# Idle TensorE products in pairs, the first keys fetched before the first queries, and a new table of order

## The chip, the cores and the metric

The kernel runs on one core of a Trainium2 chip. The metric is the device time of one execution in microseconds (us). Three executions of the kernel before took 779.79, 780.46 and 781.97 us, so the median is 780.46 us. A profiled execution has its own time, given below.

## The reference

Hashed attention over 2 batches, 8 heads, 768 positions and a head width of 64, followed by two feed-forward layers on the 1536 resulting tokens, all in 32-bit floats:

```
q_bits, k_bits = (q @ proj > 0), (k @ proj > 0)        # 6 bits each -> a bucket number
scores = where(q_bucket == k_bucket, q @ k.T / sqrt(64), -1e9)
attn   = softmax(scores);  x = attn @ v                # tokens x 512
h = x @ w_in;  g = h if h >= 1, 0 if h <= -1, else (h + 1)**2 / 4
y = g @ w_out                                          # 512 -> 2048 -> 512
out = ((y @ w_a) * (y @ w_b)) @ w_out2                 # 512 -> 1536 -> 512
```

## The kernel before, in words

Every 32-bit operand of a large product is split into a high and a low part, and three products stand for one (high by high, high by low, low by high). The split is two instructions: a rounding copy (line L372 on VectorE and GpSimd, L370 on ScalarE) and a subtraction (L375 on VectorE or GpSimd).

Attention of batch 0 runs first, in tiles of 128 queries by 768 keys. For each head: load the keys (`kn`, L395) and queries (`qnh`, L384); copy the keys beside themselves (`kn<-kn`, L372); split the queries (`qsh`); transpose keys (`tk`, L488) and queries (`tq`, L528) on TensorE and evict them (`kh`, `kl`, `qt`); form the hash signs (`kp`, L561; `bit`, L566) and the bucket rows (`kid`, L579, L613, L614; then `q2`, printed as `q`, L622, and the upper half of `kl`, L588). A tile of scores is four products (`s`, L673), a row minimum on VectorE (`mn`, L677) and an exponential on ScalarE (`sm`, L679). It is then split into `phi` and `plo`, turned by DMA (L707) and multiplied by the values in groups of 36 products (`pv`, L746). There are 96 tiles and 48 groups of values.

As soon as blocks of 384 tokens of batch 0 are complete (`xn`), they are transposed (`xt`, L1012), split into `xsh` and `xsl`, and the first feed-forward layer starts (`hp`, L1044; `acc`, L1256). Its products fill TensorE between the attention tiles of batch 1. The second layer follows (`mx`, `mz`, `acc`, L1177, and the output product L1282). Weights arrive as raw words (`stage`, L937) and are put together on ScalarE and VectorE (`wab`, `F`, L940 to L946).

Nothing schedules this at run time. Every step is recorded as an operation with the engines that may take it. The string `ORDER` gives, for each operation in turn, the engine (p, a, v, g or s) and the distance in the list to the next operation. It therefore fixes the order on each engine's queue, and which engine takes a step that several can take. Each engine runs its queue in order. SyncE (SP) issues the DMAs, also in order. Buffers are handed out from pools in that same order: `kn` has one buffer, so the next head's keys can be requested only when both `tk` steps of this head are done.

At the start TensorE gets products that compute nothing (`idle<-warm`): eight at L1340, and eight more from `keep_busy` (L473), which `tq` calls around the first head's query transposition. In the kernel before, the latter are two operations, one of six products and one of two. The first score tile of the program is recorded as waiting for these operations (`after=idle_mm`).

Of the kernel before, what the change touches and what calls it, by code (L numbers as in the profile page):

```python
# [39 lines left out]
a46 v19 v17 s-49 a38 a24 p-23 a-11 p16 v p v2 g15 a-16 s-23 p9 a10 v-3 g-15 p39 a g-23 g13 v11 p a v p-17 v a-12  # L40
p36 a58 g2 a-59 v136 s-184 s201 a68 p-227 a-18 a48 v-7 g8 s-72 v184 v-165 v23 v112 p-106 s-9 g a9 s-24 p3 v s-3
p50 v v a-51 a18 g-1 g9 v-75 p95 a v-44 a13 g13 a198 p-194 a v14 s174 a-187 g3 p-15 v p244 p-237 v v237 v v-277
a32 g17 p-12 p32 a s-11 a p-14 v4 g14 s-30 a196 v-183 p55 a v p-43 v a119 a-133 p51 a-36 s8 p a a24 g v133 v-131
v v81 v a-116 g11 p-4 p5 a p a a s-48 p33 v7 s-10 p47 a p-26 s18 v-28 v13 v-2 a-12 p38 v-29 g8 a52 s-79 g80 a100
s-40 p-99 v a7 p13 p2 v-1 v3 v-1 a-42 s2 p3 v a16 s-19 g18 a-1 a17 p-6 g-14 p41 a a59 v-86 a v-26 v53 p g-27 g20
s24 s-43 p16 v s-16 a26 v p-25 p26 v v54 a-66 g2 g12 p9 a v31 g g-63 p35 p108 a-119 s448 v-398 a-54 a19 p-6 v111
p-119 v11 v2 g17 s-33 a12 p6 v105 p-103 a2 a-1 v-2 p28 v a22 g p-41 g-1 a-14 v60 p-22 a g-18 s-35 s94 v-64 a p10
v p-6 v v p47 s-52 a12 g-1 g13 p-3 v a-12 g17 p2 s-28 v29 p a31 v g-5 v-26 a-9 v11 a g12 v-53 a119 a-60 p-9 v
p-17 a5 p26 a p10 v s50 a v p-33 v-26 v60 v-33 s-66 a21 s8 p11 v v26 p-20 a-22 a19 a33 v s-77 p25 g17 v7 s-27
a19 a11 p31 p-5 v6 p s-62 p30 a33 p34 v-41 a v-33 a v6 v p46 v s42 a-17 g-46 g-51 p37 a v g13 g46 s-78 a95 v v  # L50
s-31 a5 v-17 a-1 v-15 a29 v v s-68 a56 v18 p-55 a a-15 g a15 v p16 p33 a-32 a a35 g6 p-24 a s-4 v-31 v p37 p26
a-28 g v-19 p58 s32 a v-60 a a-31 g298 s-285 a47 g a-19 v49 v a-46 v12 s8 a p-31 v a v-37 v74 v-7 v p-48 a26 v
s-8 a36 g20 p-26 a p-51 p2 p43 p-1 s-5 a45 s-63 a40 g p-10 v a s59 v-28 s-99 p56 p p14 v p-23 v s56 a-69 v p49
a6 v20 a-70 g p71 v-27 a28 a41 g a-30 s-37 s-18 p21 s-2 a3 a-6 g25 a-113 v128 p-52 a a a28 v23 v17 p-37 p11 g27
v-37 a v-32 v28 a-27 g p35 a a4 p9 p-28 s50 v-19 s p5 p-38 s57 v-85 v35 v28 g8 p-41 p a14 a22 v-9 a s3 s40 p-38
a-38 v20 a19 p3 v a-20 v a30 g-8 s19 v-1 v-9 g-54 a43 v-19 g v30 p14 a p11 a a-11 p-11 v v11 a-13 p-8 p33 a v-90
a67 g4 v33 a-32 v p-19 p-1 p2 a23 g p27 a-1 s-17 a-7 p20 v p-7 a-4 g p25 v35 v-70 v a20 v4 s-37 p26 a19 v a2
s-21 a17 p-6 v a g9 v v16 a-38 v33 g s-9 s117 v-141 p28 v p-34 v6 p-7 a47 p-56 a a52 p-4 v a-13 a3 v34 a-23 v-10
p13 a p6 p19 a v-54 v15 p24 a s-39 s34 a47 v-71 v19 a25 v g27 p-52 p p s15 p-4 a-8 s23 p6 a v-15 p-9 v3 p32 v-34
# [207 lines left out]
def attn_moe_kernel(ctx: ExitStack, tc: tile.TileContext, q, k, v, proj,  # L267
                    w_in, w_out, w_a, w_b, w_out2, consts, codes, out):
    nc = tc.nc
# [20 lines left out]
    HJ = J // 2  # L290
# [41 lines left out]
    add = pr.add  # L332
# [19 lines left out]
    warm = const.tile([128, 1], BF16, name="warm")  # L352
# [112 lines left out]
    busy = {}  # L465
# [932 lines left out]
```

## Time and profile before

| | |
|---|---|
| median of three runs | 780.46 us |
| the profiled execution's own time | 783.63 us |
| its span, first to last instruction | 781.8 us |
| TensorE busy | 755.3 us, 97% |
| VectorE busy | 666.1 us, 85% |
| ScalarE busy | 488.6 us, 62% |
| GpSimd busy | 374.5 us, 48% |
| mean granted TensorE clock | 0.993 of full speed |

Busy is time in which an engine executes. Times of rows are counted from the start of the span. In a row of the timeline, the square bracket says how long the engine sat idle before the row and which instruction ended that. PE is TensorE, DVE VectorE, ACT ScalarE, POOL GpSimd, and SPq is SyncE issuing a DMA.

### The profile page before, as it was taken

To read this page: it belongs to the slowest core of one execution; us is meant where nothing else is said; L and a number is where in the kernel's file an instruction comes from. 1 tells how busy PE (TensorE), PEld (TensorE's weight loads), DVE (VectorE), ACT (ScalarE), POOL (GpSimd) and SP (SyncE) were. 2 spreads that over 40 slices of the span, in tenths; PEclk is the share of its full clock that TensorE was granted. 3 is DMA by queue.
4 is the path that set the end of the run, shared out by engine and by line. 5 is a ranking of instruction groups with operands and counts; after the bars stand their busy time and mean duration, and the time that the engine had idled before them with its cause. 6 is when DMAs were issued, how large, how long until landed. Compare 5 with 4: busy or idle time off the path is not lost.

```text
span 781.8 us, 14714 instructions
## 1 busy us (share of the span) xinstructions
PE 755.3 (97%) x5532; PEld 698.5 (89%) x5532; DVE 666.1 (85%) x1176; ACT 488.6 (62%) x897; POOL 374.5 (48%) x333
## 2 busy tenths in 40 slices
PE   7888799999999999999999999999999999999998
PEld 5677699999989999989999999999999889999986
DVE  5999999999988888889977776899889996988764
ACT  5897799899998886766435433464546663443223
POOL 1667566445584667662234235253143165543630
PEclk9999999999999999999999999999999999999999
DMA  7899999999989867773022321023531103122011
GB/s 240 179 208 219 200 247 239 221 233 223 206 170 179 160 133 110 124 112 95 29 76 59 108 82 54 27 82 111 152 114 55 40 1 95 55 89 73 1 41 40
DMA packets 202791, 95.50 MB, mean 122 GB/s; under 512 B 165216, under 2 KB 197216, under 8 KB 202720
## 3 DMA queue, kind: packets, MB, share of 16 engines
q1 hardware_dynamic: 202272, 94.39, 53.0%
q8 instruction: 43, 0.70, 0.4%
q14 instruction: 28, 0.23, 0.1%
q10 hardware_dynamic: 448, 0.17, 0.1%
HBM read 53.65 MB, written 3.15 MB: 73 GB/s over the span
## 4 chain that ended last, share of the span: by engine, by line
PE 81%; DVE 11%; ACT 4%; issue 3%; DMA 1%; POOL 0%; SPq 0%; DVEq 0%; ACTq 0%; POOLq 0%
PE hp L1044 16%; PE acc L1256 15%; PE acc L1282 12%; PE mx L1177 12%; PE s L673 7%; PE mz L1177 6%; PE pv L746 5%; PE acc L1177 3%; DVE mn L677 2%; PE kp L561 2%; ACT sm L679 1%; DMA kn<-in_k 1%; PE tq L528 1%; DVE plo L375 1%; PE tk L488 1%
## 5 line engine op out<-in xcount | busy, mean ns | idle before, releaser
L375 POOL TENSOR_TENSOR plo<-sm,phi 128x768 f16<-128x768 f32 x55 | 95.0, 1730 | 33.9 <-ACT phi L370 24.1
L677 DVE TENSOR_REDUCE mn<-s 128x1 f32<-128x768 f32 x96 | 91.2, 952 | 15.8 <-PE s L673 14.9
L679 ACT ACTIVATE sm<-s,mn 128x768 f32<-128x768 f32 x96 | 86.2, 899 | 24.6 <-DVE mn L677 20.1
L1230 ACT ACTIVATE t<-hp,half 128x384 f32<-128x384 f32 x64 | 36.9, 577 | 62.4 <-PE hp L1044 61.8
L673 PE MATMUL s<-kh,qt 128*128 128x384 f32 x192 | 72.5, 378 | 2.5 <-ACT sm L679 2.1
L375 POOL TENSOR_TENSOR wlo<-F,whi 128x512 fp32r<-128x512 f32 x39 | 54.0, 1385 | 41.9 <-ACT whi L370 22.5
L673 PE MATMUL s<-kl,q 128*128 128x384 f32 x192 | 66.8, 348 | 0.5 <-DVE q L622 0.5
L1282 PE MATMUL acc<-whi,gl 128*128 128x512 f32 x144 | 56.7, 394 | 0.0
L1282 PE MATMUL acc<-wlo,gh 128*128 128x512 f32 x144 | 56.6, 393 | 0.0
L1282 PE MATMUL acc<-whi,gh 128*128 128x512 f32 x144 | 56.0, 389 | 0.0
L375 POOL TENSOR_TENSOR gl<-t,gh 128x384 fp32r<-128x384 f32 x23 | 27.8, 1207 | 55.8 <-DVE gh L372 46.4
L1044 PE MATMUL hp<-xsh,whi 128*128 128x384 f32 x152 | 51.8, 341 | 1.5 <-DVE xsl L375 1.2
L1256 PE MATMUL acc<-gh,whi 128*128 128x384 f32 x144 | 51.8, 360 | 0.0
L746 PE MATMUL pv<-vc,pth 128*128 128x65 f16 (+1 forms) x1152 | 51.2, 194 | 0.1
L1044 PE MATMUL hp<-xsh,wlo 128*128 128x384 f32 x152 | 50.9, 335 | 0.0
L1044 PE MATMUL hp<-xsl,whi 128*128 128x384 f32 x152 | 50.9, 335 | 0.0
L746 PEld LDWEIGHTS <-pth 128*128 128x128 f16 x1152 | 41.9, 98 | 7.4 <-issue 6.5
L1256 PE MATMUL acc<-gl,whi 128*128 128x384 f32 x144 | 48.4, 336 | 0.0
L1256 PE MATMUL acc<-gh,wlo 128*128 128x384 f32 x144 | 48.4, 336 | 0.0
L1239 DVE SCALAR_TENSOR_TENSOR t<-t,hp 128x384 f32<-128x384 f32 x64 | 35.1, 548 | 15.2 <-ACT t L1235 12.2
L370 ACT ACTIVATE whi<-F 128x512 fp32r<-128x512 f32 x71 | 44.2, 624 | 3.6 <-issue 1.7
L370 ACT ACTIVATE phi<-sm 128x768 f16<-128x768 f32 x53 | 44.1, 841 | 1.5 <-DMA pth<-phi 0.9
(257 smaller groups left out, 2547.1 us busy)
## 6 DMA issues: line engine op xcount, KB each, us to landing
stage<-in_moe_w_out SPq DMA_DIRECT2D x31, 512.0 KB, 4.2
stage<-in_moe_w_a SPq DMA_DIRECT2D x17, 512.0 KB, 3.6
stage<-in_moe_w_b SPq DMA_DIRECT2D x17, 512.0 KB, 3.6
stage<-in_moe_w_in SPq DMA_DIRECT2D x16, 512.0 KB, 4.4
kn<-in_k SPq DMA_DIRECT2D x16, 192.0 KB, 3.7
out<-ob SPq DMA_DIRECT2D x12, 256.0 KB, 2.1
vn<-in_v SPq DMA_DIRECT2D x4, 384.0 KB, 5.1
vscan<-in_v SPq DMA_DIRECT2D x4, 384.0 KB, 4.5
```

What stands on the lines that cost most here:

```text
L370: nc.scalar.activation(dst, src, ACTF.Copy)
L375: (nc.vector if e == "dve" else nc.gpsimd).tensor_tensor(dst, a, b, ALU.subtract)
L673: nc.tensor.matmul(s()[:, i, 0:HC], x()[:, qs], t[i]()[:, 0:HC], start=(n == 0), stop=(n == 1))
L677: add({"dve": c_dve(S)}, lambda e: nc.vector.tensor_reduce(mn(), s()[:, :, 0:HC], AX.XY, ALU.min), r=[s], w=[mn])
L679: o = add({"act": c_act(S, True) + 0.093}, lambda e: nc.scalar.activation(sm().rearrange("p (c n) -> p c n", c=2), s()[:, :, 0:HC], ACTF.E ...
L746: nc.tensor.matmul(o[:, t, 0:D + 1 - i], w()[:, t, c, :], vcs[t]()[:, c, (1 - i) * D:(2 - i) * D + 1 - i], start=(n == 0), stop=(n == 3 * ...
L1044: nc.tensor.matmul(o()[:, 0:TB], a()[:, kk, :], m(), start=(n == 0), stop=(n == 3 * KD - 1))
L1177: nc.tensor.matmul(view()[:, 0:TB], a()[:, sl], m(), start=(start and n == 0), stop=(n == 5), skip_group_check=not start)
L1230: add({"act": 0.465}, lambda e: nc.scalar.activation(t(), o()[:, 0:TB], ACTF.Relu, bias=half, scale=0.5), r=[o], w=[t])
L1239: add({"dve": c_dve(TB)}, lambda e: nc.vector.scalar_tensor_tensor(t(), t(), 1.0, o()[:, 0:TB], ALU.min, ALU.max), r=[o], w=[t])
L1256: nc.tensor.matmul(ac()[:, 0:TB], a()[:, d, :], x(), start=(f == 0 and n == 0), stop=(f == F1 - 1 and n == 2))
L1282: nc.tensor.matmul(ac(), a()[:, ts], x().rearrange("p k n -> p (k n)"), start=(f == 0 and n == 0), stop=(f == F2 - 1 and n == 2))
```

## The change

`keep_busy` now records one operation for every two idle products, so that each pair has its own place in the table. The counts fall from six and two products to three pairs and one pair, which is the same eight products. Everything else is the new table.

```diff
-    NB1, NB2 = 6, 2
+    NB1, NB2 = 3, 1
...
         def mm(e):
-            for i in range(n):
-                nc.tensor.matmul(busy["t"][:, i % 2], warm.to_broadcast([128, 128]), warm.to_broadcast([128, 512]),
+            for i in range(2):
+                nc.tensor.matmul(busy["t"][:, i], warm.to_broadcast([128, 128]), warm.to_broadcast([128, 512]),
                                  start=True, stop=True)
-        idle_mm.append(add({"pe": 0.22 * n}, mm, w=[zz], after=[after]))
+        for i in range(n):
+            idle_mm.append(add({"pe": 0.44}, mm, w=[zz], after=[after]))
...
-s3 v3 v p10 s-16 v a17 v-14 p6 p-3 a v a2 p4 s11 v-14 v15 s3 a s-28 v40 s250 p-274 a p-3 p6 a2 p-4 v v2 g20 a250
+s s2 v3 v p12 a2 v-19 p9 s18 s4 v-28 p3 p8 a-4 v a-4 v p12 s-18 v42 p-29 g30 v-17 p-12 a5 p3 v8 v-6 a-1 p-3 v
```

The table is new from its first entry to its last (3512 entries before, 3514 now). TensorE executes the same products. In the whole program the copy `kn<-kn` goes from 10 times on GpSimd, 5 on ScalarE and 1 on VectorE to 5, 9 and 2; `phi` from 28, 53 and 15 to 22, 63 and 11; `plo` from 55 on GpSimd and 41 on VectorE to 58 and 38. The new source is one line longer in the table and one in `keep_busy`, so line numbers below grow by one or two.

On TensorE at the opening, from the key transposition of the first head (`tk`) to that of the second, the kernel before has the following (of each run of like rows, one stands):

```order
L488 MATMUL tk<-cst,kn 128x128 x6
L473 MATMUL idle<-warm 128x512
L561 MATMUL kp<-qt,zq_h 103x384
L561 MATMUL kp<-kl,zk 103x384
L473 MATMUL idle<-warm 128x512
L579 MATMUL kid<-bit,code 128x384
L614 MATMUL kid<-bit,code 64x384
L488 MATMUL tk<-cst,kn 128x128 x6
```

Here the first idle row stands six times and the second twice. Now the same place reads:

```order
L490 MATMUL tk<-cst,kn 128x128 x6
L474 MATMUL idle<-warm 128x512
L563 MATMUL kp<-qt,zq_h 103x384
L563 MATMUL kp<-kl,zk 103x384
L474 MATMUL idle<-warm 128x512
L581 MATMUL kid<-bit,code 128x384
L616 MATMUL kid<-bit,code 64x384
L474 MATMUL idle<-warm 128x512
L490 MATMUL tk<-cst,kn 128x128 x6
```

The idle rows stand two, four and two times. Four of the six products ahead of `kp` moved: two to the place behind it, and two behind the last `kid`, ahead of the second head's transposition.

On SyncE the program of before begins with:

```order
L384 DMA qnh<-in_q 128x192
L395 DMA kn<-in_k 128x6x64
L414 DMA vn<-in_v 128x2x384 x2
L384 DMA qnh<-in_q 128x192
L937 DMA stage<-in_moe_w_in 128x4x256
L395 DMA kn<-in_k 128x6x64
```

It now begins with:

```order
L396 DMA kn<-in_k 128x6x64
L385 DMA qnh<-in_q 128x192
L415 DMA vn<-in_v 128x2x384 x2
L385 DMA qnh<-in_q 128x192
L939 DMA stage<-in_moe_w_in 128x4x256
L396 DMA kn<-in_k 128x6x64
```

The first two have changed places; the next four stand as they did. On VectorE the first queries are still split before the keys are copied.

On VectorE, where the second piece of the first token block is split (`xsh`, `xsl`), the kernel before has:

```order
L372 CAST xsh_1219<-xt 128x384
L677 TENSOR_REDUCE mn<-s 128x1
L375 TENSOR_TENSOR plo<-sm,phi 128x768
L375 TENSOR_TENSOR xsl_1220<-xt,xsh_1219 128x384
L622 TENSOR_SCALAR q_1286<-kid,cst 128x384
L542 TENSOR_SCALAR qt<-tq 128x384
```

Now there is:

```order
L645 SCALAR_TENSOR_TENSOR vc<-vn,up_69,vc 128x6x64 x2
L373 CAST xsh_1227<-xt 128x384
L376 TENSOR_TENSOR xsl_1228<-xt,xsh_1227 128x384
L679 TENSOR_REDUCE mn<-s 128x1
L590 TENSOR_SCALAR kl<-kid 64x384
L544 TENSOR_SCALAR qt<-tq 128x384
```

The row minimum and the subtraction `plo` no longer stand between the two halves of the split; two subtractions for the values (`vc`) stand ahead of it.

## Rows read from the trace of the kernel before

**Rows 1.** Windows: start:end, length, each engine's busy us, clock, DMA share, GB/s.
```profile
0.00:20.00 20.00, 15.11 (x63) 10.05 (x63) 12.09 (x37) 11.84 (x23) 3.58 (x9) 0.91 0.74 235
20.00:97.00 77.00, 64.94 (x686) 52.26 (x686) 72.39 (x114) 63.81 (x108) 51.30 (x49) 0.96 1.04 203
97.00:125.00 28.00, 28.00 (x264) 26.38 (x265) 27.28 (x40) 26.13 (x49) 17.31 (x13) 1.00 1.10 245
125.00:600.00 475.00, 469.67 (x3624) 447.74 (x3621) 409.88 (x733) 309.69 (x568) 223.69 (x195) 1.00 0.56 126
600.00:782.00 182.00, 177.57 (x905) 162.07 (x903) 144.48 (x256) 77.14 (x153) 78.59 (x68) 1.00 0.14 47
```

**Rows 2.** Timeline of PE: start, length, row, idle before.
```profile
11.94 1.54 PE L488 MATMUL tk<-cst,kn 128*128 128x128 f32 x6 [1.49 <-POOL kn L372]
...
20.00 0.52 PE L488 MATMUL tk<-cst,kn 128*128 128x128 f32 x3 [1.20 <-POOL kn L372]
...
72.87 0.30 PE L528 MATMUL tq<-eye,qsh 128*128 128x128 f32 x1 [2.03 <-DVE xsl L375]
...
86.54 0.55 PE L1012 MATMUL xt<-cst,xn 128*128 128x128 f32 x3 [1.43 <-DVE q L622]
```

**Rows 3.** Windows, the stretch behind the first of these.
```profile
11.98:15.39 3.41, 3.41 (x14) 3.41 (x15) 2.18 (x5) 1.86 (x5) 0.00 (x0) 0.50 0.51 171
```

**Rows 4.** Line L677 with who waits for whom on DVE, 20 to 97 us: total, times, longest.
```profile
DVE mn L677 <- PE s L673: 1.6, 4, 1.0
```

**Rows 5.** The opening: chain of waits, PE timeline, SyncE timeline, landing times of `qnh`.
```profile
1.19 3.71 DMA kn<-in_k
...
1.19 0.66 SPq L395 DMA_DIRECT2D kn<-in_k  x1
...
DMA to landing us min/median/max: 2.0/3.8/4.7
...
5.34 0.87 PE L488 MATMUL tk<-cst,kn 128*128 128x128 f32 x6 [0.28 <-DVE kn L372]
...
7.70 0.43 PE L561 MATMUL kp<-qt,zq_h 128*103 128x384 f32 x1 [0.18 <-DVE kl L375]
...
9.67 0.32 PE L579 MATMUL kid<-bit,code 103*128 103x384 f16 x1 [0.22 <-ACT bit L566]
```

**Rows 6.** Lines of DVE, 20 to 97 us: count, busy, mean ns, idle before.
```profile
L375 DVE TENSOR_TENSOR plo<-sm,phi 128x768 f16<-128x768 f32 x6 | 8.4, 1405 | 0.0
...
L946 DVE SCALAR_TENSOR_TENSOR F<-stage,F 128x512 int32<-128x512 int32 x7 | 4.7, 682 | 0.1
L622 DVE TENSOR_SCALAR q<-kid,cst 128x384 fp32r<-128x384 f32 x6 | 4.0, 669 | 0.1
...
L372 DVE CAST phi<-sm 128x768 f16<-128x768 f32 x4 | 2.7, 667 | 0.0
...
L372 DVE CAST kh<-tk 128x384 fp32r<-128x384 f32 x4 | 2.2, 542 | 0.2 <-PE tk L488 0.2
...
L542 DVE TENSOR_SCALAR qt<-tq 128x384 fp32r<-128x384 f32 x2 | 1.1, 557 | 0.7 <-PE tq L528 0.6
...
L372 DVE CAST qsh<-qnh 128x192 fp32r<-128x192 f32 x1 | 0.3, 337 | 0.0
```

**Rows 7.** Line L431 on DVE: ns min/median/max, first and last start.
```profile
L431 DVE TENSOR_REDUCE vam<-vscan x1: 939/939/939, 121.2 to 121.2; 128x1 f32<-128x768 f32 x1
```

**Rows 8.** Timeline of DVE and POOL at 69 us.
```profile
69.07 0.94 DVE L677 TENSOR_REDUCE mn<-s 128x1 f32<-128x768 f32 x1
69.94 2.32 DVE L375 TENSOR_TENSOR plo<-sm,phi 128x768 f16<-128x768 f32 x1
...
69.81 1.64 POOL L375 TENSOR_TENSOR plo<-sm,phi 128x768 f16<-128x768 f32 x1 [0.61 <-ACT phi L370]
```

**Rows 9.** Timeline of DVE and PE around the sixteenth group of values.
```profile
119.52 0.55 DVE L1239 SCALAR_TENSOR_TENSOR t<-t,hp 128x384 f32<-128x384 f32 x1
...
124.35 0.53 PE L746 MATMUL pv<-vc,pth 128*128 128x65 f16 x12
```

More of the change, by code (lines that the diff above doesn't have):

```diff
@@ L40 @@
[L40 to L59, printed above, removed]
@@ new lines @@
+v-14 a p24 a s-8 v-3 a v142 a-145 v7 g10 v172 p-170 v g18 p-17 v2 a-1 p-8 v g3 p24 a v p-5 a-56 g2 a55 v70 p-102
+p19 v163 g-160 v11 a-25 v12 a182 p-158 a a24 a-53 v54 v-94 v41 a4 p18 s159 s-200 p48 a p-21 v14 v-13 g-2 a18
+a221 s-227 g p36 a v p-5 a v p-25 v g-7 g9 a-10 p17 a2 a-1 s-36 a27 s197 a p-192 v p30 v65 p-88 s-40 p31 v33 p2
+a-29 g-7 a14 v-3 g2 g15 p-3 v170 v-221 s49 a s-26 a14 g19 v165 a-159 v-11 g-62 p102 a v p-5 a v a-38 p212 p-201
+v g11 p-5 a2 s-48 p33 s3 a26 g-20 v v12 p-11 a3 g16 p14 v s-48 v80 g a-66 p7 p27 a67 v a-106 a17 v-5 v-44 v190
@@ new lines @@
+s-168 p28 v a20 p15 v g-86 a44 g21 a g12 s-18 v a26 p-25 v p20 v148 s-185 a38 a-20 s97 g-80 p-6 v v-25 p54 a v
+a-30 p25 a s-56 g51 a g12 p-16 v a p-15 v150 p-112 a s s-43 a73 g v-15 p-30 a6 s448 a p-438 v-21 p19 v-14 a p123
+v-193 s40 p35 a9 p8 p-2 a-1 a33 v-22 v94 v v-109 v7 p26 a-25 g-6 v32 v3 v g-19 s-33 a19 a-4 p15 v p22 a-17 p6 v
+s-42 p36 a110 a-93 p9 g-18 a-13 a14 v24 s25 v-24 g-13 v6 s-30 p21 a-11 p42 a5 g v-36 a5 a26 v-49 a19 a12 v-30
+p26 p28 a s-59 p27 v-33 v37 v2 g13 p-3 v p25 v s50 a v a-61 v p27 v-26 s-39 v99 a-91 a13 p19 v s-12 a48 v-11
@@ new lines @@
+a25 p-11 v p-13 a50 v-26 g27 s-81 a44 a-10 p-3 p9 v s66 p-78 v6 v p-4 s15 p106 a-104 v-162 g p175 a v-14 p22 p2
+a80 v a-107 p25 a-18 p50 v a-37 p-4 v p100 a v a-110 v p16 p20 v-35 g11 a-4 p17 v-16 a165 v s-158 a34 p-49 s40
+g-45 p56 s-24 a5 g v-9 s151 a-140 a v v-11 s2 p24 v-97 g a134 v a-66 p22 a p11 v p4 a-63 a37 a-9 v36 v-15 p26
+g-37 p59 a-82 v v a43 a-20 v v v19 a a14 p-47 a a84 p-61 a24 s-23 a18 g43 p-49 v p59 a p-28 p-47 p46 a-30 v10 a
+v33 v-39 v-4 p59 g-54 p22 s-15 a118 a-105 a35 s-59 p39 v a-55 a58 v-33 s27 v-12 v-39 v a98 s-84 p14 a a-4 a203
@@ new lines @@
+a-174 p19 a v-48 v v67 s-29 p-6 a g v17 a4 g p-8 v v-14 v a18 v40 p-17 p-9 v2 p-11 p p-2 a-8 a25 v a-7 a9 a-39
+p18 v-17 v p31 g-35 p69 v10 a-37 v p27 a-34 p18 a4 g4 s-83 p89 a-31 v18 v-89 a21 v178 p-137 a-48 v v a74 p15
+a-42 a15 g s-30 p80 a v g-32 s-49 a50 g a16 p-24 v p16 a v7 g-117 p113 v v p3 a-24 v42 a g19 p-23 v a-15 a v
+s-64 a v a76 a-13 g p39 a p-10 s-56 p45 v-82 v94 s46 a128 p-178 s-71 p66 p-2 v-3 a-60 v v v78 s-64 g234 a-175 g6
+g-76 a66 a42 a-29 p14 p-40 a p5 p32 v3 a a35 g6 s-64 p52 a-32 p13 a-1 v-24 a s-8 s-34 v35 v23 v-1 a10 a-66 v67
@@ new lines @@
+p24 a p-45 v38 a a11 v-96 v a74 v-60 a32 p30 v126 v-117 v-10 s-97 a v v67 p20 a s-43 s-21 a65 a42 p-52 v-78 a75
+p4 v-20 g17 v55 a-35 a s-59 p39 p3 p30 v v-13 a-59 v a72 v-71 g-17 a75 v p37 a g a-24 g p39 a p-35 v a p-5 p p
+v20 v17 s-52 v19 p-7 s-11 p54 v a4 g a-39 v14 g g21 p8 a p-29 p25 a-6 s61 a93 v-172 v p25 p-38 a v a30 p11 v
+s-116 a v v g4 p61 a a48 p-10 p6 a p-25 a v p18 s-44 a62 s-29 s-32 a33 a-24 p11 v v p51 v g-19 a22 a52 p-58 a
+s198 s-217 g-1 v139 s-137 p2 v a18 a3 p-52 a a63 v-62 g-18 p53 v129 a79 g-141 p-51 a a-16 p5 v12 g-19 a42 g-28
@@ new lines @@
+p22 v a a11 s82 v-123 g-105 p126 v p-27 s37 p-18 v9 s61 v-72 g19 s2 a-18 a p21 v a v-22 a p33 g-11 v-27 v189
+p-160 p-7 a17 a s-7 p-49 a77 v-29 v-2 s4 g-28 g56 a-39 v18 a-10 a5 p15 v v p13 p-10 v p-9 a v a8 a-73 p59 v g-10
+v169 p-137 v p a-27 s12 v151 s2 p-135 v a-13 a-77 s93 a-6 v-11 a19 a-4 p-9 g-28 p56 v-18 s2 v12 a14 g-60 a51 a-4
+p-11 a v15 v-120 v121 s19 a-16 a-44 a245 p-237 p23 v a p37 v-149 p169 g-31 s2 v-139 v324 g a-156 v p-63 a66 v
+p-87 p47 v g5 g12 a-44 p15 p42 v-40 a-1 a42 p-20 p p-2 v22 a-53 g p12 v v15 a-23 a16 a17 g4 p-16 a a-13 g-8 p28
@@ new lines @@
+g-65 v14 v81 a71 a-100 p-55 v a g50 p76 v-72 a v-42 v43 g27 p-87 v p6 v p27 a96 a g-126 s5 a25 v122 p4 v-34
+v-171 g53 s2 a-3 a4 a21 p-20 v v51 p-36 v a p127 p-122 p123 v-27 a-95 s5 a2 v89 g-101 g-75 p203 g-119 s2 p-5 v a
+a283 v-195 p-78 a p-6 a125 g v-37 p41 p-3 v-109 v g15 p-19 v264 v-263 a p102 s-84 p93 g-215 a88 a119 a-83 v80 g
+g-69 v72 v p-91 a92 p-85 a p-18 a2 a-1 p107 a2 v-99 p101 a-100 v91 a-100 a110 v-132 v2 a131 p-110 a2 s9 g14 s5
+g-1 s2 a83 g p3 p v-118 p20 g-43 v129 p9 v-94 a p94 v3 a-88 p v78 a g p-87 v a a6 v87 g-82 s5 v-6 p84 a a p-89 v
@@ new lines @@
+p12 p-10 p-1 p17 a182 s-214 a v a25 v v v p6 p-3 v-30 v28 p4 p16 p-2 p-15 p14 p2 a68 s-140 a v v229 v-228 a56 a
+v a251 a-250 p12 g-11 a771 v-725 s-43 a v p15 v112 v-126 a6 a v a g v154 p-152 p7 a s-45 a p37 p14 v178 a-40
+a-56 a-88 v p4 p-15 p17 p g137 v-56 p-85 a-2 g g182 p-169 p4 v99 a-110 a v a v135 s-153 p21 a6 g-8 p4 p12 p-15
+p13 p-1 v-70 a66 a126 v-125 v-66 v192 p-119 v-6 v156 g v-156 p3 p9 a-6 g151 g-131 s43 a92 g a-155 v151 v-150 a
+p6 p-4 p3 g-4 p12 a-6 p-3 a-43 p54 v-53 a86 p-30 v31 v107 v g-149 v a g p p2 p12 v-63 a56 g v v v p15 v189 a-73
@@ new lines @@
+a13 v31 v3 s a-8 p-18 a27 v-8 v-27 v-13 v-13 s71 a v p2 a2 v-15 v-5 v6 v31 v-90 g3 a7 g v-32 v53 p-13 v4 v v46
+a-35 v56 p-93 v3 p35 a p-3 v4 a46 v a11 p-36 v2 a-12 v13 g v22 g2 g v-2 s11 g-85 v84 s12 v-58 p24 a2 a22 p-60 p
+p38 p35 p-52 a49 a5 p-43 p-31 p42 v-18 v35 v11 v g16 v-27 a31 v-53 p38 a2 p-43 p5 v-15 g64 v-246 g247 g-2 p-9
+v14 v-60 p28 v2 a p9 v-20 p-12 g24 v-26 v15 a73 p-65 v4 p48 v-39 a20 v g-4 p-15 a3 p23 v-22 v4 v20 v v-20 a-35 g
+s47 p5 a-4 v v6 a-10 v v10 v-6 a14 p2 p-3 v2 s-7 a p45 v2 v-46 v-18 v19 g16 g2 p-49 v50 s20 a-32 p a p-3 p-36
@@ L156 @@
+v v15 a-9 p4 v6 p-4 p7 v3 v a-10 p4 g-10 p17 v-52 v p45 p7 p v-12 v15 v p3 p-1 a-12 v a15 v p-6 v3 v9 v p-4 p-2
+a-11 v p11 p7 p-1 v5 v-15 v16 p-4 p7 p-1 p-1 v-4 v a6 v a-15 v p17 v v p-4 p11 a s p-8 a p-5 p7 a s-2 s3
 """
```

174 lines of the change are left out of this document (74 added, 100 removed).

## The prediction

> **What bounds the kernel now.** I read the windows first [rows 1]. TensorE is busy 15.11 of the first 20 us, 64.94 of the next 77, and all 28.00 of 97 to 125. After that it lacks 5.3 us in 475 and 4.4 in the last 182. So some 17 of its 27 idle us lie ahead of 97 us, where no work of the feed-forward layers fills the gaps between attention tiles. There VectorE is the engine to look at: 72.39 of 77 us busy. From 97 to 125 both are full (28.00 and 27.28 of 28). What shifts the end is therefore the moment at which TensorE comes out of this opening, plus any later wait that changes.
>
> TensorE's timeline [rows 2] then tells what ended its longer gaps: 1.49 us at 11.94 (keys copied on GpSimd), 2.03 at 72.87 (VectorE's `xsl`) and 1.43 at 86.54 (VectorE's `q`). Behind the first the granted clock is 0.50, level 1.2 of 2.4 GHz, for 3.41 us [rows 3]; behind the gap of 1.20 us at 20.00 I take it as unchanged, since the mean of 20 to 97 us, 0.96, is what two more such stretches make (2 × 3.41 × 0.5 / 77 = 0.044). Each stretch costs at most 3.41 / 2 = 1.7 us of TensorE's work.
>
> The profiled execution took 783.63 us (span 781.8 and 1.83 around it), 3.17 above the median of 780.46. I work out a shift of the profiled execution and carry it over to the median.
>
> **The idle pairs.** Before, six products stand ahead of `kp` and `kp` still waited 0.18 us for `kl` [rows 5]: they lay under that wait, and taking four away gives nothing. The pair added ahead of `kid` costs about a row's 0.43 us (the likest row in [rows 5], `kp` of 384 columns) against a wait of 0.22 us there: 0 to 0.2 us, taken as 0, since what follows waits for the second head's keys anyway. The last pair now stands in the 1.49 us gap and cuts it into pieces of about 1 us or less, below the 1.20 that left the clock up. So the first slow stretch should go: bounds 0 and 1.7 us, taken 1.7, for it follows the gap directly.
>
> **The keys first.** Before, `kn` was issued at 1.19 and landed 3.71 us later; `tk` began at 5.34, 0.28 us after TensorE ran dry, on VectorE's copy of the keys [rows 5]. The issue of `qnh` ahead of it now comes second; taking 0.45 us for that issue (an estimate, below the 0.66 of the row for `kn`), the keys land at 0.74 + 3.71 = 4.45. The queries are issued at about 1.4; with landing times of 2.0 to 4.7 us they are there between 3.4 and 6.1. VectorE still splits the queries ahead of copying the keys, so late queries hold the keys back. `tk` comes between 0.4 us earlier and 0.7 later; I take 0.4 later, nearer to the late end, since the median landing (3.8) puts the queries at 5.2. That passes on to the second head, whose keys can be requested only after both `tk` steps.
>
> The Trainium skill (DMA: Bandwidth & Descriptors, section "Queues, rings and completion order") says that each DMA engine works through its descriptors in ring order. By it the queries would not land ahead of the larger keys, which speaks against the swap: 0.7 instead of 0.4. No row of before has this order, so none shows it.
>
> **VectorE up to the first hidden product.** I counted VectorE's rows ahead of the first L1044 in both orders: 130 and 130, of other kinds. Prices are from [rows 6, 7].
> - Fewer: 2 `plo` × 1.405, 4 `kh` × 0.542, 2 `q` × 0.669, 2 `kl` at the price of `kh` (like shape) × 0.542: 2.81 + 2.17 + 1.34 + 1.08 = 7.40.
> - More: 2 `phi` × 0.667, 2 `vam` × 0.94, 2 `qt` × 0.557, and a `kn` copy and two steps on `qsh`, less one on `vc`, 2 × 0.337: 1.33 + 1.88 + 1.11 + 0.67 = 4.99.
>
> The sum is −2.4 us. The steps that left go to ScalarE and GpSimd, busy 63.81 and 51.30 of 77 us [rows 1]; that room is the cover. Without it the 2.4 are lost.
>
> **VectorE up to the sixteenth values group.** The group starts at 124.35, and the last VectorE row that it depends on before, the `t` at 119.52, ends at 120.07 [rows 9]: 4.3 us to spare. In the new order this group takes the bank that the fifth L1239 frees, so it follows VectorE directly. Up to that `t` VectorE has 163 rows before and 170 after. More: 3 `phi` 2.00, 4 `vam` 3.76, a row minimum 0.94, 2 `qt` 1.11, two steps of weights (L946) 1.36; fewer: 4 `kh` 2.17, a `q` 0.67, 2 `kl` 1.08; the rest cancels. That is +5.25. Neighbours overlap by 0.07 us (the row minimum at 69.07 lasts 0.94, the next starts at 69.94 [rows 8]), so seven more rows cost 0.5 less: +4.8 us.
>
> Against it stands the idle time that VectorE gets back. In the opening: 1.7 of the clock less 0.4 of the late keys, 1.3. At 70 us `plo` stood between `xsh` and `xsl`; it took 2.32 us while GpSimd ran a `plo` of its own from 69.81 to 71.45 [rows 8], and TensorE waited 2.03 for `xsl`. With it moved, scores come earlier; VectorE waited 1.6 us for scores in four places, the longest 1.0 [rows 4]; bounds 0 and 1.6, taken 1.0. The third gap (before 86.54, for `q`) is taken to stay. VectorE's row then ends at 120.07 + 4.8 − 1.3 − 1.0 = 122.57, and the group starts 1.8 us before 124.35. TensorE alone could be there at 124.35 − 2.4 − 2.3 = 119.65: most of what the opening gains is given back to VectorE between 97 and 125 us. These 2.9 us I take as spread over the banks that the five `t` steps free, in waits too short to lower the clock.
>
> The Trainium skill (SBUF — State Buffer, section "Who interferes with whom") says that a VectorE instruction with two SBUF inputs and a GpSimd instruction reading SBUF shut each other out. The rows agree: 2.32 us here beside a GpSimd `plo`, against a mean of 1.405. By it two more `plo` on GpSimd ahead of the first hidden product would cost VectorE up to 2 × (2.32 − 1.405) = 1.8 us, and the gain would be 0, which is B's time and counted there.
>
> **Later waits** (5.3 us from 125 to 600) I take as unchanged, for the table reorders all of them without aim that I can read from rows; bounds: half of them gone (−2.7), or doubled (+5.3).
>
> **The forecast (A).** 783.63 − 1.8 = 781.8 for the profiled execution, 780.46 − 1.8 = 778.7 for the median. Own range 777 to 780.
>
> **Rivals.**
> D: all three slow stretches go. The third is worth the 0.6 us that [rows 4] leave to VectorE (1.6 − 1.0), and with it 1.0 of the later waits goes: −3.4, 777.0. For it: two of three gaps wait for VectorE rows that others overtake now. Against: `q` still stands behind a `plo` there.
>
> B: ScalarE takes it back between 125 and 200 us. Up to the 24th group of values it has 287 rows in the new order and 277 before; at its mean of 26.13 / 49 = 0.53 us [rows 1] that is 5.3 us, and from 97 to 125 it is already busy 26.13 of 28. From the point at which its lead is under that, the gain is 0: 780.5. Against: from 125 to 600 it is busy only 309.69 of 475.
>
> C, slower: VectorE recovers no idle and sets the sixteenth group. Its row ends at 120.07 + 4.8 + 0.4 = 125.27, so the group is 0.9 us late. TensorE could be there at 124.35 − 2.4 + 0.4 = 122.35; if the 2.9 us of wait come in one piece, longer than the 1.43 of [rows 2], the clock falls for 3.41 us, +1.7 more. Together +2.6: 783.1. It decides from the point at which VectorE's row ends after 124.35, that is, when less than about 0.5 us is recovered. For it: VectorE is 27.28 of 28 us busy there and gets more rows. Against: 7.9 us of its idle time lie in the first 20 us.
>
> That the pairs don't do what they say: the second head's keys come later by up to 0.7 us, and the gap behind the last pair stays at 1.43 or more. Then the first stretch stays, −1.8 turns into −0.1; this I count within B.
>
> **How the numbers follow.** 0.3% is 2.3 us, about what a measurement of this kernel can tell from no change: faster is below 778.1, slower above 782.8. A has 0.38 (0.16 of it faster, 0.22 within), D 0.26 (0.25 and 0.01), B 0.12 (0.11 within, 0.01 slower), C 0.24 (0.02 within, 0.22 slower). Faster is 0.41, the same 0.36, slower 0.23. The range reaches from half of the later waits gone on top of A (778.7 − 2.7, with D's remaining 1.6 it is 774.5) to C with 0.7 us more from the late keys: 774.5 to 783.8. A doubling of the later waits lies outside.
>
> **What would show it.** Right: a clock of 1.00 from 12 to 15.4 us; TensorE's first `tk` at 5.7; a wait ahead of the first query transposition near 70 us below 1 us; the first L1044 between 92 and 95 us; VectorE's last row ahead of the sixteenth group ending at about 122.6 and the group starting at once; TensorE below 28.00 busy from 97 to 125. Wrong: queries that land with or behind the keys and a `tk` after 6.0; a slow stretch at a new place; VectorE's row after 124.35 (C); ScalarE named as releaser of TensorE's waits from 125 to 200 (B); waits after 125 us that add up to much other than 5.3 us.

## The result and the profile after

The changed kernel is slower: 789.77 us (median of four runs, 789.12 to 790.71) against 781.19 for the kernel before (four runs as well, 779.79 to 781.97). The ratio is 1.0113, 95% interval 1.0093 to 1.0133, that is +8.6 us where −1.8 was forecast and the range ended at 783.8. The two profiles show 5.5 us of it (spans 787.3 and 781.8), because the profiled execution of the kernel before was itself 2.4 us above that kernel's median and that of the changed kernel 0.65 below its own.

The windows of the changed kernel (start:end, length, each engine's busy us with its instructions, TensorE's clock, DMA share, GB/s):

```profile
0.00:20.00 20.00, 15.49 (x69) 8.55 (x69) 12.67 (x34) 10.83 (x22) 2.47 (x8) 1.00 0.74 217
20.00:97.00 77.00, 63.45 (x680) 51.62 (x680) 70.81 (x117) 66.42 (x115) 55.18 (x46) 0.96 1.07 209
97.00:125.00 28.00, 28.00 (x273) 26.39 (x274) 27.65 (x42) 23.88 (x44) 13.68 (x14) 1.00 1.04 241
125.00:600.00 475.00, 465.20 (x3581) 441.43 (x3578) 401.29 (x698) 311.70 (x566) 241.17 (x209) 1.00 0.56 125
600.00:788.00 188.00, 183.68 (x940) 168.15 (x938) 152.88 (x284) 76.08 (x152) 69.19 (x63) 1.00 0.15 48
```

Against [rows 1]: up to 97 us TensorE is idle for 18.1 us instead of 17.0, but has two slow clock stretches (3.41 us at the lower clock level) instead of three. The two differences nearly cancel, and the first feed-forward product, the "first hidden product" of the predictions, begins at the same time in the kernel before and in the changed one:

```profile
96.90 0.44 PE L1044 MATMUL hp<-xsh,whi 128*128 128x384 f32 x1 [1.17 <-DVE xsl L375]
```

```profile
96.82 0.45 PE L1046 MATMUL hp<-xsh,whi 128*128 128x384 f32 x1 [0.72 <-DVE xsl L376]
```

So the opening brings none of the forecast gain. From 125 to 600 us TensorE is idle for 9.8 us instead of 5.3, and the growth lies ahead of 400 us (8.7 instead of 3.4; behind it 1.1 instead of 2.0). The waits of TensorE between 125 and 400 us (sum, times, longest) tell it best. First those of the kernel before, then those of the changed one:

```profile
PE s L673 <- ACT sm L679: 1.7, 1, 1.7
PE kid L579 <- DVE q L608: 0.2, 1, 0.2
PE tq L528 <- ACT kl L586: 0.2, 1, 0.2
```

```profile
PE s L675 <- ACT sm L681: 1.8, 2, 1.5
PE pv L748 <- DVE q L610: 1.7, 2, 0.9
PE s L675 <- DVE kl L590: 0.9, 1, 0.9
PE pv L748 <- DVE kl L376: 0.8, 1, 0.8
PE hp L1046 <- DVE q L610: 0.8, 1, 0.8
PE tk L490 <- DVE qt L544: 0.6, 1, 0.6
PE tq L530 <- DVE tl L373: 0.6, 1, 0.6
PE tk L490 <- ACT kn L371: 0.5, 1, 0.5
```

One long wait has become nine of 0.5 to 1.5 us. They end at 199, 225, 244, 250, 290, 293, 317, 324 and 339 us.

What such a wait hangs on can be read from the engines' timelines. The one at 324 us (rows of GpSimd, VectorE, ScalarE and TensorE in order of time):

```profile
319.86 1.66 POOL L376 TENSOR_TENSOR plo<-sm,phi 128x768 f16<-128x768 f32 x1 [3.35 <-ACT phi L371]
319.91 1.83 DVE L373 CAST q<-qt 64x384 fp32r<-64x384 f32 x1
...
321.77 0.96 DVE L679 TENSOR_REDUCE mn<-s 128x1 f32<-128x768 f32 x1
...
322.82 0.90 ACT L681 ACTIVATE sm<-s,mn 128x768 f32<-128x768 f32 x1 [2.31 <-DVE mn L679]
...
323.77 0.44 PE L675 MATMUL s<-kh,qt 128*128 128x384 f32 x1 [1.55 <-ACT sm L681]
```

The copy of 64 x 384 numbers on VectorE lasts 1.83 us; the same copy took 0.36 elsewhere. It ends 0.22 us after the GpSimd subtraction that began 0.05 us ahead of it. The row minimum behind it, the exponential and the next scores are all late by as much. The wait at 290 us has the same cause and a second one:

```profile
286.81 2.06 POOL L376 TENSOR_TENSOR plo<-sm,phi 128x768 f16<-128x768 f32 x1
...
287.28 1.62 DVE L768 TENSOR_SCALAR r<-tl,up 128x6 f32<-128x6 f32 x1
...
288.94 0.19 DVE L769 RECIPROCAL r<-r 128x6 f32<-128x6 f32 x1
289.05 0.51 DVE L610 TENSOR_SCALAR q<-kid 64x384 fp32r<-64x384 f32 x1
...
289.61 0.52 PE L748 MATMUL pv<-vc,pth 128*128 128x65 f16 x12 [0.90 <-DVE q L610]
```

A step on 128 x 6 numbers, 0.23 us in the median, lasts 1.62 us beside `plo`. The eviction `q` behind it frees a bank of the pool `p`, and the values wait for that bank at the head of TensorE's queue. A product `acc` whose operands were complete at 284 us stands two places behind.

Counted over all rows of VectorE from 155 to 330 us (a step counts when it lasts over 0.15 us longer than the median of its like, that is, of all steps of its line, tiles and shape in the trace): 16 steps and 6.8 us too long in the kernel before, 26 steps and 14.0 us in the changed one.

### The profile page after: what moved, and what is told of

It reads as the page before. It is cut to its first block, busy times and chain, and to the rows that moved or that the text cites. A ratio compares the mean times of both kernels' runs of the same rounds, so it can differ in the third digit from the quotient of the medians.

```text
span 787.3 us, 14720 instructions
## 1 busy us (share of the span) xinstructions
PE 755.8 (96%) x5532; PEld 696.1 (88%) x5532; DVE 665.3 (85%) x1171; ACT 488.9 (62%) x896; POOL 381.7 (48%) x336
## 4 chain that ended last, share of the span: by engine, by line
PE 77%; DVE 11%; ACT 6%; DMA 3%; issue 2%; POOL 1%; SPq 0%; ACTq 0%; POOLq 0%; DVEq 0%
PE hp L1046 15%; PE acc L1258 14%; PE acc L1284 12%; PE mx L1179 12%; PE mz L1179 6%; PE s L675 6%; PE pv L748 5%; PE acc L1179 3%; DVE mn L679 2%; ACT sm L681 2%; PE kp L563 1%; DMA kn<-in_k 1%; PE tq L530 1%; DVE F L948 1%; PE tk L490 1%
## 5 line engine op out<-in xcount | busy, mean ns | idle before, releaser
L376 POOL TENSOR_TENSOR plo<-sm,phi 128x768 f16<-128x768 f32 x58 | 100.7, 1740 | 40.8 <-ACT phi L371 25.7
L675 PE MATMUL s<-kh,qt 128*128 128x384 f32 x192 | 70.5, 367 | 4.4 <-ACT sm L681 4.2
L376 POOL TENSOR_TENSOR wlo<-F,whi 128x512 fp32r<-128x512 f32 x41 | 57.0, 1393 | 34.5 <-ACT whi L371 24.1
L376 POOL TENSOR_TENSOR gl<-t,gh 128x384 fp32r<-128x384 f32 x31 | 36.1, 1166 | 49.0 <-ACT gh L371 31.8
L371 ACT ACTIVATE phi<-sm 128x768 f16<-128x768 f32 x63 | 52.8, 841 | 0.7
L942 ACT ACTIVATE wab<-stage 128x512 f32<-128x512 f32 x55 | 36.2, 665 | 17.5 <-DMA stage<-in_moe_w_b 3.9
```

Of the source, the lines that this page charges most:

```text
L371: nc.scalar.activation(dst, src, ACTF.Copy)
L376: (nc.vector if e == "dve" else nc.gpsimd).tensor_tensor(dst, a, b, ALU.subtract)
L675: nc.tensor.matmul(s()[:, i, 0:HC], x()[:, qs], t[i]()[:, 0:HC], start=(n == 0), stop=(n == 1))
L942: add({"act": 0.556}, lambda e: nc.scalar.activation(ab(), t()[:, :, :, 1].bitcast(F32), ACTF.Prelu, scale=SHIFT, alpha=SIGN), r=[t], w=[a ...
```

## The experiments

All kernels below compute the whole reference and differ in the table of order alone. Ratios are to the kernel before on the same chip.

**The words of the change, one by one.** First the pairs alone, in the order of the kernel before:

```diff
-tk x6, idle x6, kp x6, idle x2, kid, tk
+tk x6, idle x2, kp x6, idle x4, kid, idle x2, tk
```

> The order of the kernel before, with the eight idle products alone placed as in the changed kernel (two ahead of kp, four ahead of kid, two behind the last kid). Theory 1 (the pairs are harmless, and what was lost comes from the order of the steps behind the opening): the slow stretch of 3.41 us at 12 us goes, worth 0 to 1.7 us; the time is 779.0 to 781.2. Theory 2 (the pairs hold up the second head and cost time): slower than before by 1 us or more, 782 and above.

Measured: 1.0002 (0.9989 to 1.0016). No cost or gain of the pairs can be told from this. The trace has no slow stretch at 12 us, as theory 1 says, but has others at 27, 85 and 334 us, and a second execution of the kernel before, further down, has none at 12 us either. Then the keys first alone:

```diff
-DMA qnh<-in_q; DMA kn<-in_k
+DMA kn<-in_k; DMA qnh<-in_q
```

> The order of the kernel before, with the first two requests of SyncE alone exchanged (keys ahead of queries). Theory 1: the first key transposition comes about 0.5 us later (5.8 instead of 5.33), and at most that is left at the end: 780.5 to 781.8. Theory 2 (the keys first are what costs: the later queries hold up the first head and every head behind it): 785 or above.

Measured: 1.0012 (0.9998 to 1.0026), as theory 1 has it: about +0.9 us, not told apart from 0. The first key transposition began at 5.74.

**The table, cut in two.** A joined order takes the first part from one table and all remaining steps from the other.

```diff
-one table
+steps of table 1 up to its first hidden product, then the others in the order of table 2
```

> The order of the changed kernel up to its first hidden product (a position that both reach at 96.9 us), and from there the remaining steps in the order of the kernel before. Theory 1 (the loss lies behind 155 us, in the order there): 779 to 782, with TensorE's waits from 125 to 400 us back near the 2.7 us of the kernel before. Theory 2 (the opening with its pairs, early keys and other engines leaves the later steps in a worse state, for instance ScalarE behind): 786 to 790, with waits of some 8 us there.

> The order of the kernel before up to its first hidden product, and from there the remaining steps in the order of the changed kernel. Theory 1 (the loss lies behind 155 us): 787 to 791, with TensorE's waits from 125 to 400 us near the 8.2 us of the changed kernel. Theory 2 (the opening is at fault): 779 to 782.

Measured: 1.0042 (1.0027 to 1.0057) with the changed opening, 1.0073 (1.0053 to 1.0092) with the changed rest. The window from 155 to 330 us shows which table brings the loss there. In this order: the kernel before, the changed opening with the old rest, the changed kernel, the old opening with the changed rest:

```profile
155.00:330.00 175.00, 173.41 (x1729) 160.37 (x1727) 155.23 (x263) 149.79 (x264) 107.80 (x89) 1.00 0.88 172
```

```profile
155.00:330.00 175.00, 173.39 (x1729) 160.38 (x1729) 155.83 (x262) 149.87 (x265) 108.16 (x88) 1.00 0.88 174
```

```profile
155.00:330.00 175.00, 167.18 (x1629) 153.00 (x1626) 154.01 (x249) 144.31 (x250) 109.82 (x92) 1.00 0.87 172
```

```profile
155.00:330.00 175.00, 167.21 (x1628) 153.29 (x1626) 152.90 (x248) 144.44 (x251) 110.94 (x92) 1.00 0.86 169
```

TensorE's 173.4 or 167.2 busy us come with the rest of the table, whatever stood ahead of it; the nine waits came back one by one with the same lengths (0.78, 0.77, 0.52, 0.79, 0.88, 0.65, 0.63, 1.54, 0.85). So theory 1 holds for the larger part, some 5.7 of 8.6 us (of which a wait of 0.6 us just behind the seam may be the seam's). The kernel with the changed opening was slower than theory 1 allowed, by some 2 us. Its trace has two waits just behind the seam that neither parent has:

```profile
PE pv L747 <- DVE t L1240: 1.5, 1, 1.5
PE acc L1257 <- DVE gh L372: 0.6, 1, 0.6
```

So of its 3.3 us the seam itself costs up to 2.1, and what the opening costs is not known from this kernel. A second cut was to tell it without that seam:

> The order of the changed kernel up to its eighteenth group of values (154 us, where its trace stood 1.0 us ahead of the kernel before), and from there the remaining steps in the order of the kernel before. Theory (up to 154 us the change gains or loses nothing that can be told, all of the loss lies behind): ratio 0.998 to 1.002. Rival (the steps up to 154 us leave ScalarE or the buffers in a state that costs later, as in the kernel that was joined at 97 us): 1.003 to 1.006.

Measured: 1.0037 (1.0021 to 1.0054), within what the rival says and outside the theory: the steps ahead of the seam do cost something. In the trace the seam lies at about 141 us on TensorE, not at 154, and there is no wait of 0.3 us or more between 98 and 337 us, so here the loss is not a wait at the seam.

The traces of all kernels bound the cost of the opening, if those with equally many slow stretches ahead of the first hidden product are compared. With two (each of 3.41 us; some follow each other directly), that product begins at 95.5, 96.4 and 97.0 us in three kernels with the old order of the opening (pairs moved, unchanged, keys first) and at 96.1, 96.8, 97.4 and 97.8 in four with the changed one. With one, it begins at 92.7 and 94.2 against 94.4 and 94.6. The changed opening is later by about 1 us on average, though single kernels overlap.

**The queries first again,** in the changed kernel:

```diff
-DMA kn<-in_k; DMA qnh<-in_q
+DMA qnh<-in_q; DMA kn<-in_k
```

> The changed kernel with the first two requests of SyncE alone exchanged back (queries ahead of keys). Theory (the early keys are what makes the opening later, by about 1.2 us up to the first hidden product, where both kernels are read at the same number of slow clock stretches): the first query transposition starts near 4 instead of 5.4 us, the first hidden product comes 1 us earlier than in the changed kernel, and the ratio to the kernel before is 1.009 to 1.011. Rival (other steps of the opening set it, such as ScalarE's further copies of the keys): no change, ratio 1.011 to 1.013.

Measured: 1.0083 (1.0067 to 1.0099) against 1.0113, a little more than expected, but the two intervals overlap. The first query transposition begins at 4.04, as the theory says. The first hidden product doesn't bear the theory out: it begins at 95.12 with one slow stretch, where the two mended kernels below, whose opening is the changed one with the keys first, have it at 94.42 and 94.62 with one. So the two kernels that exchange these requests put the early keys at 0.1 and 0.3%, 1 and 2 us, by their times, and a cost of that size is likely but not shown.

**Mending the waits.** The three drawn-out steps first, in the changed kernel:

```diff
 VectorE, 287 us
-r, r, q, kl, mn
+q, kl, mn, r, r
 VectorE, 315 us
-gl, tl, mn
+tl, gl, mn
 VectorE, 320 us (now on ScalarE)
-q<-qt
```

> The changed kernel with three steps of VectorE placed otherwise, those that its trace shows drawn out beside a GpSimd instruction directly ahead of a wait of TensorE: the copy q (1.83 us at 319.9) goes to ScalarE, the pair r (1.84 us at 287.3) behind the next row minimum, the subtraction gl (1.91 us at 315.0) behind the copy tl. Theory C (the loss from 155 to 330 us comes mostly from VectorE steps drawn out beside GpSimd): the waits of 0.90, 1.55 and 0.64 us go, and the time falls by 2 to 3 us against the changed kernel, to a ratio of about 1.008 to the kernel before. Rival (these waits only cover others of the score chain, which is late anyway): less than 1 us, 1.010 to 1.013.

Measured: 1.0058 (1.0036 to 1.0081), below the whole interval of the changed kernel. The three waits are gone, so theory C has their cause right. But one of the others, ahead of the transposition at 291 us, grew from 0.6 to 1.8:

```profile
PE tk L490 <- DVE qt L544: 1.8, 1, 1.8
```

Then the order at the heads of the queues alone:

```diff
 ScalarE, 198 us
-gh, kl
+kl, gh
 ScalarE, 225 us
-wab, kl
+kl, wab
 TensorE, 243 us and 292 us
-tk, acc
+acc, tk
 TensorE, 339 us
-s, acc, acc
+acc, acc, s
```

> The changed kernel with the order alone mended at five of its waits, no engine changed: at 198 us ScalarE evicts kl ahead of the split gh, at 225 us kl ahead of wab, and at 243, 292 and 339 us one or two products acc that are ready stand ahead of the TensorE step that waits. Theory O (the loss is that a step which waits stands at the head of a queue while ready ones stand behind it): about 3 us fall away (0.5, 0.76, 0.48, 0.5 and 0.87), ratio about 1.007 to 1.008. Rival (the score chain sets the pace, the idle time moves to a later place): under 1 us, 1.010 to 1.013.

Measured: 1.0066 (1.0044 to 1.0087), a time as theory O has it. In the trace the five waits are gone, but TensorE's waits for the exponential, 1.8 us in two places in the changed kernel, have become:

```profile
PE s L675 <- ACT sm L681: 3.8, 4, 1.5
```

Two of these are new (0.35 us at 296 and 0.98 at 338), and one has grown from 0.2 to 0.9 (at 228), which is what the rival says. And both:

> Both mends of the two kernels above in one. If both theories hold each for its part, 5 to 6 us fall away and what is left is the opening: ratio 1.003 to 1.006. If only one holds, the ratio is that of the better one alone, near 1.008. If neither, 1.010 to 1.013.

Measured: 1.0050 (1.0032 to 1.0068), as expected if both hold, though the three intervals overlap and the times alone don't show that they add. The traces give less than the times, and they nearly add up. From the first hidden product to the start of the 45th values group the changed kernel takes 251.7 us, with the three steps moved 250.1, with the queue heads mended 250.9, with both 249.0, and the kernel before 246.9. So in the traces the mends are worth 1.6, 0.8 and 2.7 us of the 4.8 us lost there, where the ratios differ by 4.3, 3.7 and 4.9 us from that of the changed kernel. The changed kernel was not run again beside its mends, so the rest of these differences stays unexplained. Some of each mend came back as other waits: with both, `acc` waits 1.0 us for `wlo` where `acc` was moved ahead.

**The same reading applied to the kernel before.** Its one long wait stands behind a drawn-out step as well (rows of GpSimd, VectorE and TensorE):

```profile
330.55 2.44 POOL L375 TENSOR_TENSOR plo<-sm,phi 128x768 f16<-128x768 f32 x1
...
331.37 1.90 DVE L372 CAST whi<-F 128x512 fp32r<-128x512 f32 x1
333.30 0.96 DVE L677 TENSOR_REDUCE mn<-s 128x1 f32<-128x768 f32 x1
...
335.31 0.44 PE L673 MATMUL s<-kh,qt 128*128 128x384 f32 x1 [1.72 <-ACT sm L679]
```

```diff
 331 us
-whi<-F on VectorE
+whi<-F on ScalarE
```

> The kernel before with one step given to another engine: the copy whi at 331.4 us, 1.90 us long on VectorE beside a GpSimd instruction (its like take 0.42), goes to ScalarE, which is idle from 331.42 to 334.35. It is followed by the row minimum that the one long wait of TensorE behind 100 us hangs on (1.72 us at 335.3). Theory C: this wait goes and the time falls by 1.2 to 1.8 us, ratio 0.9977 to 0.9985, faster than both kernels. Rival (the wait comes from the score chain, and moves): under 0.5 us, ratio 0.9994 to 1.0006.

Measured: 0.9970 (0.9957 to 0.9984), faster than both kernels, by 2.3 us against the kernel before. The copy took 0.61 us on ScalarE, and the wait is gone: from the start of the 44th values group to that of the 45th, between which it lay, this trace takes 10.8 us instead of 12.6. That is the 1.8 us at the upper end of theory C; the rest of the 2.3 is within the interval. A wait of 0.64 at 298 us is new here, but the next kernel, with the same order there, doesn't have it. A second mend on top:

```diff
 VectorE, 82 us
-mn, plo, vc, mn, q
+mn, mn, plo, q, vc
```

> The kernel before with whi on ScalarE at 331 us, and with four steps of VectorE at 82 to 86 us in another order: the row minimum that is ready at 82.2 us goes ahead of the subtraction plo, which took 2.02 us beside a GpSimd plo, and q, on which a TensorE wait of 1.43 to 1.73 us hangs, ahead of vc. Theory C: that wait falls to about 0.7 us or less, and with it at times a slow clock stretch behind it (up to 1.7): 0.7 to 2.4 us beyond the first mend, ratio 0.994 to 0.997. Rival (VectorE's work up to the first hidden product is what counts, not its order): as with the first mend alone, 0.997.

Measured: 0.9974 (0.9956 to 0.9991). The wait fell to 0.77 as planned, and the next transposition waits 1.18 in its place:

```profile
84.84 0.55 PE L1013 MATMUL xt<-cst,xn 128*128 128x128 f32 x3 [0.77 <-DVE q L623]
...
89.06 0.52 PE L529 MATMUL tq<-eye,qsh 128*128 128x128 f32 x3 [1.18 <-DVE qsh L375]
```

The time agrees with the rival, though its interval reaches into what theory C says, and so do the two waits: where VectorE is the bound, the new order of its steps moved the wait and didn't remove it.

**The kernel before once more,** unchanged:

> The kernel before, unchanged, profiled once more. If the slow clock stretches and the drawn-out plo at 69.94 us (2.32 us) are set by the order, they stand at the same places, at 12, 73 and 87 us. If they hang on the chance of an execution, they stand elsewhere or are fewer, and the first hidden product comes up to 5 us earlier than at 96.89.

Measured: 783.04 us, first hidden product at 96.40. The outcome is mixed. There is no slow stretch at 12 or 87 us, and one at 27 us is new:

```profile
26.95:30.36 3.41, 3.41 (x25) 3.10 (x26) 2.83 (x6) 3.41 (x6) 1.99 (x2) 0.50 1.14 206
74.73:78.14 3.41, 3.41 (x42) 3.10 (x42) 1.58 (x3) 3.12 (x5) 3.33 (x5) 0.50 1.21 234
```

The other follows the same wait as in the first execution, 2.03 us at 72.7 for `xsl`. The drawn-out `plo` ahead of it came back too, with 2.07 us, beside a GpSimd `plo` that began first:

```profile
69.68 1.64 POOL L375 TENSOR_TENSOR plo<-sm,phi 128x768 f16<-128x768 f32 x1 [0.35 <-ACT phi L370]
70.06 2.07 DVE L375 TENSOR_TENSOR plo<-sm,phi 128x768 f16<-128x768 f32 x1
```

In the kernel with the pairs moved, whose order is the same here, VectorE was first by 0.3 us. There GpSimd's step is the long one, and TensorE waits 0.20 us for `xsl`:

```profile
70.03 0.94 DVE L375 TENSOR_TENSOR plo<-sm,phi 128x768 f16<-128x768 f32 x1
70.35 2.14 POOL L375 TENSOR_TENSOR plo<-sm,phi 128x768 f16<-128x768 f32 x1 [1.06 <-ACT phi L370]
```

So the order decides which steps can meet, and tenths of a microsecond upstream decide which of the two is held up.

## Why the prediction was wrong

**The step that failed** is above all the one on the later waits, taken "as unchanged", with their doubling left outside the range. They grew by 4.5 us in the profiles, within the bound of +5.3 that I had written down. The table is new to its last entry; I worked out the first 125 us to a tenth of a microsecond and gave the other 655 one sentence. The trace of the kernel before could have said more: its one wait of 1.72 us at 335 us hung on a drawn-out step even then. The kernel has 96 score tiles, and any of them can meet a GpSimd step once the order is changed.

With these 4.5 us alone the sum would have been 783.2, still inside the range. The forecast missed by 10.4 us, and the other parts are: 1.5 us of the 1.8 that the opening was to gain and didn't (124.08 instead of 122.57 for the sixteenth values group), 3.1 for carrying a shift of the profiled execution over to the median (the profiled execution of the kernel before was 2.4 us above its median, with a third slow stretch, that of the changed kernel 0.65 below), and 1.3 behind 124 us that I can't place.

**The pairs.** The clock stayed at 1.00 at 12 us, as forecast, but not because the gap was cut. Behind the last pair TensorE still sat idle for 1.75 us, longer than the 1.49 of [rows 2]:

```profile
10.47 0.61 PE L474 MATMUL idle<-warm 128*128 128x512 bf16 x2
12.84 0.55 PE L490 MATMUL tk<-cst,kn 128*128 128x128 f32 x3 [1.75 <-POOL kn L373]
```

```profile
12.84:16.25 3.41, 3.26 (x20) 2.78 (x21) 1.89 (x3) 2.80 (x6) 0.00 (x0) 1.00 0.31 79
```

Two slow stretches stood at 29 and 49 us instead. Since the unchanged kernel had none at 12 us in its second execution, the 1.7 us that I booked for the first stretch was no property of the order. For the 1.0 us at 70 us it is a matter of chance as well: the wait of 2.03 us came back in that second execution, but neither the kernel with the pairs moved nor that with the keys first, whose order there is the same, has it.

**The keys first.** `tk` began at 5.80 (5.7 forecast). The keys landed at 3.88 and the queries, issued at 1.47, only behind them, at 4.59; VectorE split the queries and then copied the keys. The term of 0.4 was right at its place (0.46) and grew on the way: the second head's keys were requested at 7.12 us instead of 6.24 and landed at 12.15 instead of 11.19.

**VectorE up to the first hidden product.** The kinds of rows that leave and come are much as I counted them, but VectorE was busy 1.0 us less up to 97 us (83.48 instead of 84.48), not 2.4. Steps that I took as equal were drawn out in the new order: a weight step `F` took 2.14 us (0.68 elsewhere), a `vc` 1.38 (0.61), and a `qsh` 1.85 (0.35) beside a GpSimd `plo`:

```profile
42.31 1.66 POOL L376 TENSOR_TENSOR plo<-sm,phi 128x768 f16<-128x768 f32 x1
42.33 1.85 DVE L376 TENSOR_TENSOR qsh<-qnh,qsh 128x192 fp32r<-128x192 f32 x1
```

So the mechanism behind the later waits also took back part of this term.

**VectorE to the sixteenth group.** Its last row ended at 123.48, not at 122.57, and the group began at 124.08, 0.27 us earlier than before instead of 1.8:

```profile
122.93 0.55 DVE L1241 SCALAR_TENSOR_TENSOR t<-t,hp 128x384 f32<-128x384 f32 x1
```

```profile
124.08 0.53 PE L748 MATMUL pv<-vc,pth 128*128 128x65 f16 x12
```

The mechanism was right so far as VectorE takes its steps back between 97 and 125 us, but TensorE stayed at 28.00 of 28 busy, so it and not VectorE set the group. The first hidden product came at 96.82 instead of 92 to 95, for want of the idle time that was to be recovered.

**The rivals.** C had the right side and the wrong place and size. B named ScalarE behind 125 us; of the nine waits ScalarE ends two by name, and its busy time from 125 to 600 us is nearly the same (311.70 and 309.69). The collisions of VectorE and GpSimd, which I weighed ahead of 97 us only and priced by the number of GpSimd's steps, mattered all along the program: what counts is which VectorE step stands beside which GpSimd step, and who waits behind it. The Trainium skill (SBUF — State Buffer, section "Who interferes with whom") has the rule that the prediction weighed, for a VectorE step with two inputs from SBUF. Of the three drawn-out steps that waits hang on here, only the subtraction `gl` at 315 us (1.91 us, 0.56 in the median) is of that kind; the copy and the step on 128 x 6 numbers are not, and I hadn't counted such steps. The range, too, was too narrow by its own terms, since a bound that had been written down was left out of it; its lower end counts 1.0 us of the later waits twice, in the half and in D, which changes nothing here.

What stays open: the opening's share, which the traces put at about 1 us and the joined kernels at 1.2 (3.3 less the seam) to 2.9, how much of it is the early keys, and why the mends gained more in time than in their traces.

## What to carry to other kernels

Where an order is fixed in advance and engines run their queues blindly, a change of that order is to be read over the whole program, not only where it was aimed. In a profile, look behind each wait of the bound engine for a step that lasts longer than its like, and give that step to an idle engine or put it behind the step that is waited for; one such letter in the table was worth 0.3% here (0.16 to 0.43), about what the whole change was forecast to give. Of VectorE's steps, those that read TensorE's results directly were not held up here, so they are the ones to place beside a GpSimd step. A mend pays where another engine has room; where the engine that is mended is the bound, the wait comes up again one step later.

## What the runs showed of the hardware

VectorE's copies, conversions and element-wise steps whose inputs all lie in SBUF (the memory of all tiles but TensorE's results) mostly last until the GpSimd step beside them is over, or up to 0.8 us longer, when that one began first: 1.83 us for a copy of 0.36, 1.62 for a step of 0.23, 1.90 for a copy of 0.42. In the changed kernel this met 50 of 55 such steps, in the kernel before 52 of 56 (counted where GpSimd's step began over 0.02 us earlier and lasted over 0.15 us past VectorE's usual end). Steps of VectorE that read a result of TensorE were never held up in the same position, 85 in the changed kernel and 93 in the kernel before. The same line shows both. `r<-tl,up`, which took 1.62 us at 287 us, takes its numbers from a copy in SBUF; `r<-pv,up` takes them from TensorE's result:

```profile
79.83 1.66 POOL L376 TENSOR_TENSOR plo<-sm,phi 128x768 f16<-128x768 f32 x1 [0.95 <-ACT phi L371]
...
80.81 0.21 DVE L768 TENSOR_SCALAR r<-pv,up 128x6 f32<-128x6 f32 x1
```

Reciprocals, counted apart, kept their length too (6 in each kernel). The row minimum is never drawn out either, over 96 of them (ns, least, median, most):

```profile
L679 DVE TENSOR_REDUCE mn<-s x96: 936/956/960, 14.9 to 355.0; 128x1 f32<-128x768 f32 x96
```

The Trainium skill (SBUF — State Buffer, section "Who interferes with whom") says that a reduction on VectorE stays clear of GpSimd on this chip, and that a copy in its fast form, or a step with two inputs from SBUF beside a GpSimd step that reads SBUF, does not. The row minima agree, and the subtractions that were drawn out fit; whether the copies ran in that form no row shows.

TensorE's slow stretches (level 1.2 of 2.4 GHz, 3.41 us, or two back to back) were one to three per execution in the first 100 us, and their places differed in part between two executions of the same program: 12, 73 and 87 us in one, 27 and 75 in the other. Two kernels also had one behind their wait of 1.72 us at 334 or 337 us, in stretches that others with the same wait passed at 1.00.
